# Second bucket pass: the first hop's pairs in runs of 3, 3, 3 instead of 2, 2, 2, 3

## The chip, the cores and the metric

One core of one Trainium2 chip. The metric is the device time of one execution in microseconds (us), lower is better. Engines are named as the profile names them: PE is TensorE (PEld its weight loads), DVE is VectorE, ACT is ScalarE, POOL is GpSimd, SP is SyncE, which here only issues DMAs.

## The reference, cut to what matters

```python
N, deg, D = 10000, 16, 128;  E = N * deg;  K = 7
h = x;  toks = [x]
for _ in range(K):
    msg = h[src] * deg_inv_sqrt[src, None] * deg_inv_sqrt[dst, None]
    h = _segment_sum(msg, dst, N)
    toks.append(h)
tok = jnp.stack(toks, axis=1)          # (N, K+1, D)
...                                    # one attention block over the 8 tokens of a node, then a weighted sum
```

Seven times, each of 10000 nodes sums the scaled rows of the nodes that point at it (160000 edges). The eight stages of a node then go through a small attention block. The change touches only the code that does the first of the seven sums.

## The kernel before, in words

**Stages.** A first bucket pass (`pass_a`) sorts the edges by the destination's tile of 128 nodes (79 tiles). A second bucket pass builds, for each destination tile, 0/1 matrices that gather source rows and scatter them, and stores them in DRAM. The first hop is done inside this second pass, tile by tile, with the matrices just built. Hops 2 to 7 read the matrices back (`run`, L738 on), and the attention block ends the kernel.

**The second pass in quads.** Tiles go in 20 groups of four (`quads`, L694; one has three). Three Python generators are advanced in turn in a loop of 16 steps per quad (L712 to 717):

- `place` (L418) for quad q+1. For each pair of tiles DVE makes a one-hot `oh` (L426), PE adds it up over 25 chunks into PSUM `ur` (L430), ACT casts to `H` (L431), PE multiplies by triangles (L436, "U"), ACT casts to `U2` (L438), DVE forms `ux` (L226), PE adds it up (L230, L231), DVE reduces to the ranks `rk` (L234), makes the one-hot `rob` (L441) and the two products `R` (L443, L444; L219), and PE multiplies `oh` by `R` into `tb` (50 matmuls, L449), which ACT casts to `tbs` (L450). `tbs` goes to DRAM as `srow` (L459). Then the overflow: `ct`, `cnt` matmul (L477), two one-hots `ohp` (L493) with 16 matmuls each (L496), `lo` (L499), `Sov` (L503).
- `matrices` (L506) for quad q, which is one quad ahead of hop 1. For each tile it reads a row of `srow`, broadcast, as `ra` and `rb` (L517); DVE compares `rb` (L524), ACT makes the next part from `ra` (L529), DVE the rest (L532); the tile `w` is written to DRAM (L534). `rb` has one buffer: the load for the next tile is issued by SP only when L524 of this tile is done.
- `hop1` (L697) for quad q-1: one `block` (L548) per tile.

**A block.** It has nine "pairs". `gather(jj)` (L602) is 8 matmuls with 32-column weights into a PSUM tile `p` (pool of three), L608, and one eviction to an SBUF tile `eb` by ACT (L613) or, in the last quad only, every second one by DVE (L615). `scat` (L575) is 4 matmuls with 128-column weights from `eb` into the accumulator (L558, L559). Gathers are issued in runs; after a run, pending scatters are issued until two are left (`lag`), so that a scatter follows its gather by a run. The generator yields after each run. When a block's last scatter is issued, `close` (L588) adds the rows that were fetched by indirect DMA and calls `fin1` (L676): DVE copies the in-degree (L677), ACT scales (L680, L651), and each second time the new table rows are made (L164, L165, L687).

**Buffers that matter here.** In `bw1` (one buffer each) the tags `ux` and `ohp` are shared: `ux` and `R` use one buffer, `ohp` and `rob` another. `oh` has three buffers.

**What sets the order.** The program order of the three generators gives priorities; a scheduler then decides the order of instructions on each engine when the program is built. Each engine runs its own list in order.

Of the kernel before, what the change touches and what calls it, by code (L numbers as in the profile page):

```python
# [47 lines left out]
class Hops:  # L48
# [608 lines left out]
    def run(self, ctx, att, nhop=K):  # L657
        tc, nc, V, A, T, G = self.tc, self.nc, self.nc.vector, self.nc.scalar, self.nc.tensor, self.nc.gpsimd
        with ExitStack() as c:
            self.bp = c.enter_context(tc.tile_pool(name="bp", bufs=1))  # L660
            self.TT = self.bp.tile([128, NCH, NTP], F32, name="TT")
            G.memset(self.TT[:, :, NK:], 0.0)
            self.pass_a()
            self.decode()
            self.gsp = c.enter_context(tc.tile_pool(name="gs1", bufs=6))
            self.pg = c.enter_context(tc.tile_pool(name="pg1", bufs=3, space=PSUM))
            self.pacc = c.enter_context(tc.tile_pool(name="pc1", bufs=2, space=PSUM))
            self.ogp = c.enter_context(tc.tile_pool(name="og1", bufs=2))
            self.fp = c.enter_context(tc.tile_pool(name="fp1", bufs=1))
            self.pb_open(c)  # L670
            pend = []

            done, stored = [], []


            def fin1(t, s, acc):  # L676
                V.tensor_copy(self.indeg[:, t:t + 1], acc[:, 128:129])  # L677
                if not done:
                    fin1.y = self.fp.tile([128, 2, 128], F32, name="y2")
                A.activation(fin1.y[:, len(done), :], s, AF.Copy, scale=self.dis2[:, t:t + 1])  # L680
                done.append(t)
                self.token_out(1, t, s, self.ctok[0])
                n, b = len(done), t + 1
                if n == 2 or b in (NT, 4 * NG):
                    a, new = b - n, self.tab[1]
                    self.to_table(fin1.y[:, :n, :], new, self.q2, a, b)
                    V.tensor_reduce(self.mx[1][:, a:b], new[:, a:b, 0:128], axis=X, op=ALU.max, apply_absolute_value=True)  # L687
                    stored.append((a, b))
                    done.clear()
                    while len(stored) > (t != last1):  # L690
                        self.rows(1, new, *stored.pop(0), nc.sync)


            quads = [list(range(a, min(NT, a + 4))) for a in (*range(4 * NG, NT, 4), *range(0, 4 * NG, 4))]  # L694
            dsl, W = [[] for _ in quads], [[] for _ in quads]

            def hop1(q):  # L697
                for t, w in zip(quads[q], W[q]):
                    og = [self.fetch(t, j, (self.tabd[0], self.tabh[0])) for j in range(NI + 1)]
                    yield from self.block(t, w, self.tab[0], og, pend, 2, (2, 2, 2, 3), True,  # L700
                                          lambda jj: q < nq - 1 or jj % 2 == 0, fin1, t == quads[0][0])

            nq, last1 = len(quads), quads[-1][-1]
            for _ in self.place(quads[0], dsl[0]):
                pass
            for q in range(nq + 1):
                pl = self.place(quads[q + 1], dsl[q + 1]) if q + 1 < nq else iter(())
                if q == 0:
                    mt = self.matrices(quads[0], dsl[0][0], W[0])
                    next(mt)  # L710
                hp = hop1(q - 1) if q else iter(())
                for i in range(16):  # L712
                    if i % 3 != 1:
                        next(pl, None)
                    if i % 4:
                        next(mt, None)
                    next(hp, None)
                for g in (pl, mt, hp):
                    for _ in g:
                        pass  # L720
                if q + 1 < nq:
                    mt = self.matrices(quads[q + 1], dsl[q + 1][0], W[q + 1])
                    next(mt)
            while pend:
                pend.pop(0)()
        with ExitStack() as c:
# [10 lines left out]
            pend = []  # L737
            for k in range(2, nhop + 1):  # L738
                i = 1 - k % 2
# [29 lines left out]
                og = [[None] * (NI + 1) for _ in order]  # L769
# [11 lines left out]
                for n, t in enumerate(order):  # L781
                    w = self.gsp.tile([128, (NJ + NG) * 128], F8, name="w")
# [591 lines left out]
```

## Time and profile before

| | |
|---|---|
| time, median of 3 | 3912.85 us (3900.72 to 3913.69) |
| the profiled execution | 3935.55 us, of which the span from first to last instruction is 3933.8 us |
| granted TensorE clock, mean | 0.977 |
| second bucket pass with hop 1 | about 410 to 1157 us of the span |
| hops 2 to 7 | from there to about 3290 us |
| busy share of the span | PE 94%, DVE 81%, ACT 72%, POOL 43% |

The profiled execution lies 0.6% above the median. In the rows of a timeline the columns are: start in us from the span's start, duration, engine, line, operation, output and input tiles, and in brackets how long the engine sat idle before it and what released it. In the table by windows each engine has its busy time and the number of its instructions, followed by the granted clock, the DMA share and GB/s.

### The profile page before, as it was taken

The page shows a single profiled execution, that of the slowest core. Times are in us where ns is not written, and L with a number is a line of the kernel's source. Part 1 is how long each engine was busy: PE and PEld are TensorE (multiplying, and loading weights), DVE is VectorE, ACT ScalarE, POOL GpSimd, SP SyncE. Part 2 cuts the span into 40 slices and gives each one's busy share as a digit, 9 for nine tenths or more (in the row PEclk, how much of TensorE's full clock was granted, in tenths as well). Part 3 has the DMA queues.
Part 4 walks back from the last instruction along what each step waited for, and adds up shares of the span by engine and source line. Part 5 has one row for each costly group of instructions (what it writes and reads, how often), then busy time and mean ns, then how long its engine had stood idle before and what let it go on. Part 6 is the DMA issues. An engine that isn't in the chain of part 4 may idle for free.

```text
span 3933.8 us, 174231 instructions
## 1 busy us (share of the span) xinstructions
PE 3693.9 (94%) x74141; PEld 2983.6 (76%) x74141; DVE 3172.3 (81%) x6888; ACT 2812.9 (72%) x6950; POOL 1678.8 (43%) x2221
## 2 busy tenths in 40 slices
PE   6786899999989999999999999999999998999997
PEld 4665677777768888888788788888878886777775
DVE  8998999999967777777777777777776664888888
ACT  6885577777766666766666667666765667888885
POOL 0000233323236665666666566656656662121111
PEclk8898899999999999999999999999999999999998
DMA  3100454544546666666666666666666552222220
GB/s 101 38 2 1 140 168 154 163 152 161 161 150 202 202 199 194 204 199 204 188 201 201 192 201 203 198 192 199 204 192 201 187 187 92 82 77 85 77 83 19
DMA packets 332729, 595.58 MB, mean 151 GB/s; under 512 B 57447, under 2 KB 215493, under 8 KB 326693
## 3 DMA queue, kind: packets, MB, share of 16 engines
q1 hardware_dynamic: 293989, 506.70, 40.0%
q0 software_dynamic: 35392, 72.55, 6.5%
q8 instruction: 580, 9.50, 1.0%
q10 hardware_dynamic: 2560, 5.12, 0.5%
q14 instruction: 208, 1.70, 0.1%
HBM read 455.49 MB, written 128.67 MB: 148 GB/s over the span
## 4 chain that ended last, share of the span: by engine, by line
PE 75%; DVE 14%; ACT 4%; DMA 4%; issue 2%; SPq 0%; another core or an unknown queue 0%; ACTq 0%; DVEq 0%; POOLq 0%
PE p L608 27%; PE acc L583 23%; PE acc L568 4%; PE pv L1018 4%; PE pu L1002 3%; DVE ux L226 2%; DVE o L219 2%; PE po L1037 2%; PE pt L992 2%; DVE oh L213 2%; PE tb L449 2%; DVE w L532 2%; PE ps L1067 1%; DVE R L219 1%; PE acc L558 1%
## 5 line engine op out<-in xcount | busy, mean ns | idle before, releaser
L613 ACT ACTIVATE eb<-p 128x512 f16<-128x512 f32 x3065 | 1638.7, 603 | 571.0 <-PE p L608 339.1
L615 DVE TENSOR_TENSOR eb<-p,four 128x512 f16<-128x512 f32 x1912 | 1230.9, 685 | 327.5 <-PE acc L583 189.7
L608 PE MATMUL p<-tab,w 128*32 128x256 f16 x39816 | 1291.8, 274 | 39.4 <-ACT eb L613 17.4
L608 PEld LDWEIGHTS <-w 128*32 128x32 fp8e4 x39816 | 997.5, 96 | 223.8 <-issue 169.2
L583 PE MATMUL acc<-eb,w 128*128 128x256 f16 x8532 | 1014.2, 273 | 0.5 <-issue 0.3
L583 PEld LDWEIGHTS <-w 128*128 128x128 fp8e4 x8532 | 836.9, 98 | 99.8 <-issue 1.0
L544 POOL DMA_INDIRECT og<-tabh,oidx x553 | 616.9, 1115 | 655.2 <-DVE oidx L468 394.5
L544 POOL DMA_INDIRECT og<-tabd,oidx x541 | 551.8, 1020 | 739.1 <-PE acc L566 359.6
L653 POOL TENSOR_SCALAR r<-s,ctok 128x128 f32<-128x128 f32 x474 | 294.8, 622 | 44.8 <-DVE s L599 27.8
L644 ACT ACTIVATE tab<-s,c 128x128 f16<-128x128 f32 x395 | 158.5, 401 | 198.0 <-DVE eb L615 171.4
L645 DVE SCALAR_TENSOR_TENSOR tab<-s,c,tab 128x128 f16<-128x128 f32 x395 | 138.9, 352 | 180.9 <-issue 168.3
L1107 POOL TENSOR_TENSOR p<-e,in 128x1024 f32<-128x1024 f32 (+1 forms) x40 | 76.5, 1914 | 446.6 <-DVE e L1106 446.6
L1059 ACT ACTIVATE junk<-tab 128x128 f32<-128x128 f32 x626 | 248.4, 401 | 8.2 <-SPq L1343 6.8
L347 ACT ACTIVATE rs<-iof,rb 128x128 fp8e4<-128x128 f32 x784 | 231.8, 391 | 0.3
L558 PE MATMUL acc<-eb,w 128*128 128x129 f16 x1422 | 214.2, 223 | 1.0 <-ACT w L529 0.9
L532 DVE TENSOR_TENSOR w<-dsl,iof 128x2432 fp8e4<-128x2432 f16 x79 | 211.9, 2682 | 2.7 <-PE acc L559 2.7
L599 DVE TENSOR_REDUCE s<-acc 128x128 f32<-128x256 f32 x474 | 196.3, 414 | 19.9 <-issue 8.9
L559 PE MATMUL acc<-eb,w 128*128 128x128 f16 x1422 | 210.1, 220 | 0.0
L543 POOL COPY og<-eb 128x1 f16<-128x1 f16 x452 | 84.0, 186 | 254.3 <-ACT eb L613 254.3
L558 PEld LDWEIGHTS <-w 128*128 128x128 fp8e4 x1501 | 139.2, 98 | 68.0 <-issue 64.3
L1018 PEld LDWEIGHTS pv<-Wv,xT 128*64 128x64 f32 x2504 | 138.8, 137 | 44.4 <-ACT uT L1003 29.7
L1018 PE MATMUL pv<-Wv,xT 128*64 128x131 f32 x2504 | 163.1, 280 | 8.6 <-issue 3.9
(299 smaller groups left out, 5033.1 us busy)
## 6 DMA issues: line engine op xcount, KB each, us to landing
w<-gsd SPq DMA_DIRECT2D x474, 592.0 KB
gsd<-w SPq DMA_DIRECT2D x79, 592.0 KB
tok<-r SPq DMA_DIRECT2D x546, 64.0 KB
tab<-tok SPq DMA_DIRECT2D x273, 128.0 KB
tabd<-tab SPq DMA_DIRECT2D x396, 64.0 KB
ra<-srow SPq DMA_DIRECT2D x79, 320.0 KB
rb<-srow SPq DMA_DIRECT2D x79, 256.0 KB
og<-tabh,oidx POOLq DMA_INDIRECT x553
```

What stands on the lines that cost most here:

```text
L347: A.activation(ro[:, j - a, i, :], self.iof, AF.Abs_reciprocal_sqrt, scale=2.0 ** 21, bias=rb[:, j - VP, i:i + 1], saturate=False)
L532: V.tensor_tensor(w[:, :NJ * 128].rearrange("p (j d) -> p j d", d=128), dsl[:, g, :, None].to_broadcast([128, NJ, 128]), self.iof1[:, None ...
L544: self.nc.gpsimd.indirect_dma_start(out=o, out_offset=None, in_=src[0] if i == NI else src[1], in_offset=bass.IndirectOffsetOnAxis(ap=self ...
L558: T.matmul(acc[0][:, :128 + ones], W, rows[:, 128:256 + ones], start=start, stop=False, skip_group_check=True)
L559: T.matmul(acc[0][:, :128], W, rows[:, :128], start=False, stop=False, skip_group_check=True)
L583: T.matmul(acc[0][:, :256], w[:, J * 128:(J + 1) * 128], e[:, j, :256], start=False, stop=J == NG - 1 and not late)
L608: T.matmul(p[32 * q:32 * q + 32, j], w[:, NJ * 128 + s * CAP:NJ * 128 + (s + 1) * CAP], tab[:, s, :], start=True, stop=True)
L613: A.activation(e[:, :n, 0:256], pv, AF.Copy, scale=4.0)
L615: V.tensor_tensor(e[:, :n, 0:256], pv, self.four[:, :, None].to_broadcast([128, n, 256]), op=ALU.mult)
L653: self.nc.gpsimd.tensor_scalar(r, s, ct[:, t:t + 1], None, op0=ALU.mult)
L1018: T.matmul(p[64 * h:64 * h + 64, u - us[0], :], S[i]["xT"][:, h * m + q, 64 * c:64 * c + 64], Wv, start=True, stop=True, tile_position=(0, ...
L1059: A.activation(j, S[i]["x"][:, g, :], AF.Square, bias=S[i]["x"][:, g, 0:1], scale=-1.0, accum_out=R[i % 6][:, 0, g:g + 1])
```

## The change

In the first hop, the nine gathers of a block are issued in runs of 3, 3, 3 instead of 2, 2, 2, 3. A block then yields three times instead of four, and `hop1` is advanced in 12 of the 16 steps of a quad instead of in all of them. Nothing is computed differently.

```diff
             def hop1(q):
                 for t, w in zip(quads[q], W[q]):
                     og = [self.fetch(t, j, (self.tabd[0], self.tabh[0])) for j in range(NI + 1)]
-                    yield from self.block(t, w, self.tab[0], og, pend, 2, (2, 2, 2, 3), True,
+                    yield from self.block(t, w, self.tab[0], og, pend, 2, (3, 3, 3), True,
                                           lambda jj: q < nq - 1 or jj % 2 == 0, fin1, t == quads[0][0])
...
                     if i % 4:
                         next(mt, None)
-                    next(hp, None)
+                    if i % 4 != 3:
+                        next(hp, None)
                 for g in (pl, mt, hp):
                     for _ in g:
                         pass
```

Since a scheduler sets the order on each engine, the change moves more than the gathers. After some irregular first quads, the order before repeats itself quad by quad; the order of the change repeats itself every two quads, six times (quads 6 to 17). Call these two quads A and B. The three places below are all in that steady part.

DVE around the first `tb` of a quad: `R` is the last input of the `tb` matmuls, L524 is the compare of `rb`, and the 128x3800 rows are `oh` and `ux`. Before:

```order
L219 TENSOR_TENSOR R<-rob,dl 128x25x64
L454 MAX ov<-vo 128x8 x2
L524 TENSOR_SCALAR w<-rb,pid_232 128x1024
L213 TENSOR_TENSOR oh<-kB,io_230 128x3800
L226 TENSOR_TENSOR ux<-oh,U_14861 128x3800
L677 COPY indeg<-acc 128x1
L524 TENSOR_SCALAR w<-rb,pid_232 128x1024
```

The same place in the change, quad A:

```order
L219 TENSOR_TENSOR R<-rob,dl 128x25x64
L454 MAX ov<-vo 128x8 x2
L524 TENSOR_SCALAR w<-rb,pid_232 128x1024
L226 TENSOR_TENSOR ux<-oh,U_14861 128x3800
L677 COPY indeg<-acc 128x1
L524 TENSOR_SCALAR w<-rb,pid_232 128x1024
```

and quad B:

```order
L219 TENSOR_TENSOR R<-rob,dl 128x25x64
L454 MAX ov<-vo 128x8 x2
L226 TENSOR_TENSOR ux<-oh,U_15812 128x3800
L677 COPY indeg<-acc 128x1
L524 TENSOR_SCALAR w<-rb,pid_232 128x1024
```

`oh` has left this place (it now stands between `rk` and `rob` further on); `ux` follows instead, in A with one L524 ahead of it and in B with none. In A only `ux` and a copy are left between two L524.

DVE behind the second `tb`, where the matrices of the next quad begin (L532 is the long compare of `matrices`, `po` and `ph` belong to the overflow). Before:

```order
L468 TENSOR_SCALAR oidx<-msc 128x4
L532 TENSOR_TENSOR w<-dsl,iof_228 128x2432
L480 TENSOR_TENSOR po<-msc,iof_228 128x32
L524 TENSOR_SCALAR w<-rb,pid_232 128x1024
L481 TENSOR_TENSOR po<-po,fl 128x32
L483 TENSOR_SCALAR ph<-po 128x4x8
L213 TENSOR_TENSOR ohp<-ph,io_230 128x2048
L677 COPY indeg<-acc 128x1
L532 TENSOR_TENSOR w<-dsl,iof_228 128x2432
L213 TENSOR_TENSOR ohp<-ph,io_230 128x2048
```

In the change, end of quad A:

```order
L468 TENSOR_SCALAR oidx<-msc 128x4
L532 TENSOR_TENSOR w<-dsl,iof_228 128x2432
L480 TENSOR_TENSOR po<-msc,iof_228 128x32
L524 TENSOR_SCALAR w<-rb,pid_232 128x1024
L481 TENSOR_TENSOR po<-po,fl 128x32
L532 TENSOR_TENSOR w<-dsl,iof_228 128x2432
L483 TENSOR_SCALAR ph<-po 128x4x8
L677 COPY indeg<-acc 128x1
L524 TENSOR_SCALAR w<-rb,pid_232 128x1024
L213 TENSOR_TENSOR ohp<-ph,io_230 128x2048
```

The second L524 of the quad stands one L532 and three small rows behind the first; before, it came a dozen rows further on, behind `Sov`. In B the second L524 stands far behind, as it did before.

ACT around the first `tb` (`tbs` is cast when the `tb` matmuls are done, `U` when the triangle matmuls of L436 are done, `H` when those of L430 are). Before:

```order
L431 CAST H<-ur 128x152
L613 ACTIVATE eb_256<-p 128x2x256
L613 ACTIVATE eb_258<-p 128x2x256
L613 ACTIVATE eb_260<-p 128x2x256
L450 CAST tbs<-tb 76x128
L438 CAST U_14861<-ur 128x152
```

In the change, quad B:

```order
L431 CAST H<-ur 128x152
L613 ACTIVATE eb_264<-p 128x2x256
L438 CAST U_15812<-ur 128x152
L613 ACTIVATE eb_256<-p 128x2x256
L450 CAST tbs<-tb 76x128
```

PE's order is the same in this: before, L430, gathers, `tb`, scatters, triangles; now L430, triangles, gathers, `tb`. The triangles, which need `H`, have moved ahead of `tb`, in A as in B.

## The prediction

> **What bounds the kernel now.** I read the busy table first, then the windows, then the waits of the engine that looks full, then its timeline. The change can act only in the second bucket pass, so the averages of the span are not what counts.
>
> ```profile
> PE 3693.9 (94%) x74141; PEld 2983.6 (76%) x74141; DVE 3172.3 (81%) x6888; ACT 2812.9 (72%) x6950; POOL 1678.8 (43%) x2221
> ```
>
> By this PE is the fullest engine. In a window of one steady quad of the second pass (37.3 us) and one near its end, it is otherwise:
>
> ```profile
> 600.00:640.00 40.00, 37.04 (x756) 29.26 (x749) 39.66 (x55) 31.01 (x66) 17.29 (x9) 0.96 0.49 164
> 832.00:869.30 37.30, 34.97 (x718) 27.54 (x715) 34.89 (x52) 29.12 (x62) 11.45 (x8) 1.00 0.50 160
> 1125.00:1140.00 15.00, 13.55 (x283) 9.38 (x279) 5.00 (x14) 11.94 (x26) 4.03 (x6) 1.00 0.34 102
> ```
>
> DVE (third column) works 34.89 of 37.30 us with 52 instructions. PE shows as much, but the ends of its overlapping matmuls are modelled, so a full column is not a full engine; what decides is who waits. In the earlier, irregular quads (first row) DVE has only 0.34 us free in 40. At the end (third row) DVE is a third busy and PE and ACT carry the work. The steady stretch of ten quads, 740 to 1110 us, has these waits, of DVE and then of PE (total, times, longest):
>
> ```profile
> DVE oh L213 <- PE tb L449: 18.6, 17, 1.7
> DVE w L524 <- DMA rb<-srow: 5.2, 8, 1.6
> DVE oidx L468 <- ACT dsl L467: 4.1, 2, 2.1
> DVE ux L226 <- ACT U L438: 3.3, 1, 3.3
> ...
> PE tb L449 <- DVE R L219: 8.8, 11, 1.0
> PE p L608 <- ACT eb L613: 5.0, 10, 0.7
> ```
>
> DVE waits 31.2 us of 370, most of it for PE to finish the 50 `tb` matmuls, and PE in turn stands at `tb` until DVE has written `R`. One quad of DVE's timeline shows it:
>
> ```profile
> 890.15 0.68 DVE L503 TENSOR_TENSOR Sov<-lo,iof 128x512 fp8e4<-128x512 f32 x1
> 894.08 0.41 DVE L234 TENSOR_REDUCE rk<-ur 128x50 f16<-128x250 f32 x1
> 896.46 0.98 DVE L219 TENSOR_TENSOR R<-rob,dl 128x1600 f16<-128x1600 f16 x1
> 897.54 0.73 DVE L524 TENSOR_SCALAR w<-rb,pid 128x1024 fp8e4<-128x1024 f16 x1
> 899.53 2.14 DVE L213 TENSOR_TENSOR oh<-kB,io 128x3800 f16<-128x3800 f16 x1 [1.25 <-PE tb L449]
> 901.58 2.17 DVE L226 TENSOR_TENSOR ux<-oh,U 128x3800 f16<-128x3800 f16 x1
> 903.74 0.74 DVE L524 TENSOR_SCALAR w<-rb,pid 128x1024 fp8e4<-128x1024 f16 x1
> ...
> 913.21 2.14 DVE L213 TENSOR_TENSOR oh<-kB,io 128x3800 f16<-128x3800 f16 x1 [0.88 <-PE tb L449]
> 915.34 2.68 DVE L532 TENSOR_TENSOR w<-dsl,iof 128x2432 fp8e4<-128x2432 f16 x1
> 918.26 0.75 DVE L524 TENSOR_SCALAR w<-rb,pid 128x1024 fp8e4<-128x1024 f16 x1
> ...
> 927.42 0.68 DVE L503 TENSOR_TENSOR Sov<-lo,iof 128x512 fp8e4<-128x512 f32 x1
> ```
>
> From `Sov` to `Sov` a quad takes 37.27 us, of which DVE waits 1.25 + 0.88 = 2.13 us. So **DVE's own list sets the pace** of the steady quads: a quad is its work (35.1 us) plus what it waits. PE's side of the first wait:
>
> ```profile
> 894.79 1.82 PE L430 MATMUL ur<-oh,id 128*128 128x152 f16 x25
> 897.50 1.99 PE L449 MATMUL tb<-R,oh 128*76 128x64 f16 x50
> ```
>
> `R` ends at 897.44, `tb` starts at 897.50 and ends at 899.49, `oh` starts at 899.53. The L524 between (0.66 us from start to next start) only fills part of those 2 us.
>
> **The change part by part.** No engine gets an instruction more or less; DVE's 35.1 us per quad stay. What changes is how often PE turns from 32-column to 128-column weights, and the order.
>
> *Turns on PE: four per block become three.*
>
> ```profile
> 825.24 0.62 PE L608 MATMUL p<-tab,w 128*32 128x256 f16 x16
> 825.79 0.23 PE L558 MATMUL acc<-eb,w 128*128 128x129 f16 x1
> ...
> 827.50 0.22 PE L558 MATMUL acc<-eb,w 128*128 128x129 f16 x1
> 827.56 0.22 PE L559 MATMUL acc<-eb,w 128*128 128x128 f16 x1
> 827.71 0.40 PE L608 MATMUL p<-tab,w 128*32 128x256 f16 x8
> ...
> 831.21 0.84 PE L608 MATMUL p<-tab,w 128*32 128x256 f16 x24
> 831.98 0.23 PE L558 MATMUL acc<-eb,w 128*128 128x129 f16 x1
> ```
>
> From the start of 16 gather matmuls to the next scatter it is 0.55 us, of 24 it is 0.77: 0.22 us for each eight and 0.11 once. From the last scatter back to a gather it is 0.15 us, where two scatters are 0.06 apart: 0.09. A turn there and back costs 0.20 us; 79 blocks save 79 x 0.20 = 16 us of PE. **DVE's list hides it**: PE already stands waiting for `R`. Only where DVE is not the bound does it show: in about the last 45 us, of which the third window is a part, some six blocks of 7 us: 6 x 0.20 = **1.2 us gained**. The Trainium skill, "TensorEngine Tiling (Array Packing)", section "Key Properties", says that changing the tiling mode drains TensorE; the 0.20 us a turn agree with that, and by that rule alone the sum would be the 16 us of the rival below, by the waits it is 1.2.
>
> *The wait for the first `tb`.* `oh` leaves this place, but `ux` takes it, and `ux` is written into the buffer that holds `R` until `tb` has read it: the same wait, under another name. In A the L524 still stands between, so it stays about 1.25 us. In B it does not: the wait grows by its 0.66 us. **0.66 us lost per two quads.** The second wait (0.88 us) keeps the same rows ahead of it.
>
> *The distance between two L524.* `rb` has one buffer, so L524 of the next tile waits for a load that SP can issue only after this L524. What that load takes, the trace shows where L524 waited:
>
> ```profile
> 854.79 0.38 SPq L517 DMA_DIRECT2D rb<-srow  x1
> 860.58 0.75 DVE L524 TENSOR_SCALAR w<-rb,pid 128x1024 fp8e4<-128x1024 f16 x1 [0.45 <-DMA rb<-srow]
> 877.62 0.32 SPq L517 DMA_DIRECT2D rb<-srow  x1
> 881.14 0.75 DVE L524 TENSOR_SCALAR w<-rb,pid 128x1024 fp8e4<-128x1024 f16 x1 [0.47 <-DMA rb<-srow]
> ```
>
> 3.5 us on a quiet queue, 5.8 us behind other loads. Between the two L524 at the end of A stand one L532 (2.6 us) and three small rows (0.5 us): 3.1 us. Before, the next one stood behind `Sov`, more than 9 us on (918.26 to 927.42). DVE will wait 0.4 to 2.7 us; I take 1.0, nearer the short load, since the `ra` loads ahead of it are 3 us old by then. At the head of A the gap is the `tb` wait (1.25), `ux` (2.05) and a copy: 3.4 us, where it was 5.5 (897.54 to 903.74, less its own 0.66). DVE will wait 0.1 to 2.4 us; here I take 0.8. **Together 1.8 us lost per two quads.** Queued behind a waiting L524 is all of DVE's list: `ohp` and with it PE's 16 matmuls, or the table rows.
>
> Against this, some of the old 5.2 us of such waits fall in places that now have more room; I count 2 us gained once.
>
> *The order on PE and ACT.* The triangles now stand ahead of `tb`, and need `H`. From the end of `rk` (894.49), which frees `ur`, to the end of `R` is 2.95 us. In that time PE must do L430 (1.75), get `H` from ACT (about 0.45 with the latency), do the triangles (0.2) and part of a run of gathers (0.4): 2.8 us. It just fits, as it just fitted before (`tb` started 0.06 us behind `R`). I take 0, with the bounds 0 and three evictions of 0.54 us queued ahead of `H`, 1.6 us per quad.
>
> *The irregular quads before the steady part* are reordered as well. DVE is free 0.34 us in 40 there, so over some eight quads 3 us can be gained at most; lost would be 10 us, if each of them lost what a steady one does (2.46 / 2). The row with next to no free time is the nearer one, and I take 0.
>
> **The sum.** Six pairs of quads: 6 x (0.66 + 1.8) = 14.8 us lost; 1.2 and 2 gained; 11.6, say **+11 us**. The profiled execution has 3935.55 us (span 3933.8 and 1.75 around it), so 3946.6 there. It lies 0.6% above the median of the runs shown, 3912.85; since the sum is a difference, I put it on the median: **3924 us**.
>
> **The rivals.**
>
> *PE sets the pace.* For it speaks PE's 94%. Then the turns count in full: 16 us less, 3897 us. Against it: PE waits for `R`, not DVE for anything but the chain that begins with `R`. If the first `oh` wait went as well (ten quads, half of 18.6 us), 3912.85 - 16 - 12 = 3885; but `ux` shares its buffer with `R`, which forbids it.
>
> *Nothing moves.* The scheduler puts different rows at the same waits and `rb` always lands in time: 6 x 0.66 - 3.2 = +1, 3914 us.
>
> *`rb` comes late* (slower). Place: the second L524 at both spots of A. At the 5.8 us load DVE waits 2.7 and 2.4 us: 6 x (0.66 + 5.1) - 3.2 = +31, 3944 us. It decides from the point where the loads take more than about 4.9 us: then the two waits add up to 3.2 us and the loss passes 0.5%. For it: gathers by POOL and stores of 592 KB share the engines, and SP issues in order. Against it: at 903.74 a load with 5.5 us of room caused no wait.
>
> *`tb` comes late* (slower). Place: the triangles ahead of `tb`. If ACT has evictions queued ahead of `H`, DVE waits for each tenth. At the full 1.6 us in twelve quads it is 19 us more, with 0.66 kept and 1.8 halved: +25, 3938 us.
>
> **How the numbers follow.** Chances: forecast 0.45, nothing moves 0.12, PE sets the pace 0.06 and with the `oh` wait gone too 0.06, `rb` late 0.18, `tb` late 0.13. 0.5% (20 us) is about what a measurement of this kernel can tell from no change: faster than 3893, or slower than 3932. Faster: 0.06. Slower: the two slow rivals and 0.05 of the forecast's upper end, 0.36. Same: 0.58. The range leaves out the fastest case and a little beyond the slow ones: 3895 to 3952.
>
> **What would show it.** In the changed profile: `ux` (L226) instead of `oh` waits for `tb`, about 1.25 and 1.9 us in alternate quads; L524 waits for `rb` about twice per two quads with a sum near 14 us in the steady part, where it was 5.2; PE's `tb` still waits for `R`; two quads take about 77 us from `Sov` to `Sov` instead of 74.5; DVE's busy time unchanged. The prediction is wrong if PE has no wait left at `tb` (then PE leads and the turns count), if a quad is shorter than 37.27 us, or if L524's waits stay at 5 us.

## The result, and the profile after

The change takes 3919.45 us (median of 20 runs, 3908.87 to 3928.08) against 3911.36 us of the kernel before (20 runs, 3900.72 to 3913.87): a ratio of **1.0024 [1.0017, 1.0031]**, which is 6.6 to 12.1 us more. The prediction was 3924 us, 11 more than before. The profiled execution of the change took 3922.04 us (span 3920.0, clock 0.973). That of before was a long one, so the two spans can't be compared; the second pass can. The rows of the tile `Sov` give each instruction's first and last start, here of the last matmul of a block and of `Sov` itself. Before, then the change:

```profile
L566 PE MATMUL acc<-ones,Sov x79: 164/167/211, 426.0 to 1155.3; 128*128 128x1 f16 x79
L503 DVE TENSOR_TENSOR Sov<-lo,iof x20: 547/684/689, 421.0 to 1111.6; 128x512 fp8e4<-128x512 f32 x19, 128x384 fp8e4<-128x384 f32 x1
```

```profile
L566 PE MATMUL acc<-ones,Sov x79: 165/167/211, 425.3 to 1168.0; 128*128 128x1 f16 x79
L503 DVE TENSOR_TENSOR Sov<-lo,iof x20: 559/684/689, 419.1 to 1126.5; 128x512 fp8e4<-128x512 f32 x19, 128x384 fp8e4<-128x384 f32 x1
```

From the first `Sov` to the end of hop 1, which I call the **stretch** below, it was 734.3 us and is 748.9: 14.6 us more. From the last `Sov` to the end it was 43.7 and is 41.5: the tail gained 2.2. So the quads lost 16.8 us. The stretch is of one execution of each kernel: over the kernels of the table below, what it lies above that of before differs from what the ratio gives by -3 to 14 us (here 14.6 against 9.4), so smaller differences of single stretches carry little.

The waits of DVE and then of PE, 740 to 1110 us of the change (us in total, times, longest):

```profile
DVE ux L226 <- PE tb L449: 12.1, 5, 3.0
DVE w L524 <- DMA rb<-srow: 11.2, 17, 2.1
DVE oh L213 <- PE tb L449: 8.9, 8, 1.9
DVE ux L226 <- issue: 6.7, 5, 1.4
DVE lo L499 <- PE msc L496: 2.6, 4, 0.7
...
PE acc L558 <- ACT eb L613: 13.4, 10, 3.6
PE tb L449 <- DVE R L219: 12.4, 9, 1.9
PE msc L496 <- DVE ohp L213: 6.3, 5, 2.1
```

As forecast, `ux` stands where `oh` stood at the first `tb` (five times with the releaser `tb`, five times in quads A under "issue"), and the waits for `rb` have doubled. DVE waits 43.8 us in all, where it was 31.2. A row that the prediction did not have leads PE's list: scatters (`acc`, L558) that wait for an eviction, 13.4 us; before, the view had no such row. PE waits 34.3 us in all, where it was 25.3.

The timeline shows the two kinds of wait of `ux`, first in a B, then in an A:

```profile
749.20 0.98 DVE L219 TENSOR_TENSOR R<-rob,dl 128x1600 f16<-128x1600 f16 x1
753.36 2.14 DVE L226 TENSOR_TENSOR ux<-oh,U 128x3800 f16<-128x3800 f16 x1 [2.99 <-PE tb L449]
...
791.64 2.14 DVE L226 TENSOR_TENSOR ux<-oh,U 128x3800 f16<-128x3800 f16 x1 [1.33 <-issue]
```

```profile
751.21 2.05 PE L449 MATMUL tb<-R,oh 128*76 128x64 f16 x50
```

In this B, `R` ended at 750.18 and `tb` began only at 751.21, after the triangles and gathers: it is 1.03 us late on top of the forecast's 1.9. Over the five quads B the wait is 12.1 / 5 = 2.4 us; the last two of them wait 1.98 and 1.99, with `tb` 0.05 us behind `R`.

A late `rb` costs more than DVE's own wait. Of DVE, ACT and PE about 852 us:

```profile
848.81 0.32 SPq L517 DMA_DIRECT2D rb<-srow  x1
...
852.32 0.85 DVE L524 TENSOR_SCALAR w<-rb,pid 128x1024 fp8e4<-128x1024 f16 x1 [2.09 <-DMA rb<-srow]
853.19 0.14 DVE L677 COPY indeg<-acc 128x1 f32<-128x1 f32 x1
853.37 0.37 ACT L680 ACTIVATE y<-acc,dis 128x128 f32<-128x128 f32 x1 [2.60 <-DVE indeg L677]
855.00 1.57 ACT L613 ACTIVATE eb<-p 128x512 f16<-128x512 f32 x3
855.64 0.22 PE L558 MATMUL acc<-eb,w 128*128 128x129 f16 x1 [3.65 <-ACT eb L613]
856.06 1.47 PE L608 MATMUL p<-tab,w 128*32 128x256 f16 x24
```

Read it downward: L524 waits 2.09 us for `rb`; the copy of the in-degree stands behind it; ACT's L680 waits 2.60 us for that copy; the evictions stand behind L680; and PE's scatter waits 3.65 us for the first of them. With runs of three and two scatters left pending, the third scatter issued after a run belongs to that run's own first pair, so PE needs an eviction that has only just become possible. With runs of two that happens only in the run of three that ends a block.

The last row has a second surprise: 24 gather matmuls in 1.47 us, where they took 0.84. The granted clock is the number in the third column from the right. After an idle of 1.97 us that ends at 738.94:

```profile
739.00:741.00 2.00, 2.00 (x44) 1.37 (x44) 2.00 (x4) 0.92 (x3) 0.00 (x0) 0.68 0.48 161
741.00:743.00 2.00, 2.00 (x36) 1.95 (x33) 2.00 (x4) 2.00 (x4) 0.00 (x0) 0.50 0.68 238
743.00:745.00 2.00, 2.00 (x38) 1.54 (x37) 2.00 (x4) 1.51 (x5) 1.69 (x2) 0.96 0.44 178
```

```profile
738.94 0.56 PE L496 MATMUL msc<-dg,ohp 128*128 128x3 f16 x16 [1.97 <-DVE ohp L213]
739.67 1.45 PE L608 MATMUL p<-tab,w 128*32 128x256 f16 x24
```

The clock is at half for some 3 us. I summed (1 - clock) over windows of 2 us from 440 to 1156: the change loses 25.6 us of clock, before lost 8.5.

### The profile page after: what moved, and what is told of

Its sections match the earlier page's. It is cut to its first block, busy times and chain, and to the rows that moved or that the text cites. A ratio compares the mean times of both kernels' runs of the same rounds, so it can differ in the third digit from the quotient of the medians.

```text
span 3920.0 us, 174223 instructions
## 1 busy us (share of the span) xinstructions
PE 3681.7 (94%) x74141; PEld 3000.7 (77%) x74141; DVE 3163.4 (81%) x6888; ACT 2763.6 (71%) x6950; POOL 1724.6 (44%) x2221
## 4 chain that ended last, share of the span: by engine, by line
PE 66%; DMA 2%; DVE 1%; ACT 1%; issue 0%; POOL 0%; SPq 0%; POOLq 0%; ACTq 0%; DVEq 0%
PE p L608 24%; PE acc L583 23%; PE acc L568 4%; PE pv L1019 4%; PE pu L1003 4%; PE po L1038 2%; PE pt L993 2%; PE ps L1068 1%; DMA og<-tabd,oidx 1%; PE pf L1227 1%; PE sm L1074 1%; PE pf L1053 0%; DMA tabd<-tab 0%; ACT junk L1060 0%; DVE eb L615 0%
## 5 line engine op out<-in xcount | busy, mean ns | idle before, releaser
L613 ACT ACTIVATE eb<-p 128x512 f16<-128x512 f32 x3065 | 1586.7, 607 | 581.7 <-PE p L608 563.2
L615 DVE TENSOR_TENSOR eb<-p,four 128x512 f16<-128x512 f32 x1912 | 1190.5, 683 | 306.0 <-PE p L608 303.1
L608 PE MATMUL p<-tab,w 128*32 128x256 f16 x39816 | 1264.6, 275 | 8.4 <-DMA tabd<-tab 4.4
L544 POOL DMA_INDIRECT og<-tabh,oidx x553 | 641.5, 1160 | 626.5 <-DVE oidx L468 393.9
L583 PEld LDWEIGHTS <-w 128*128 128x128 fp8e4 x8532 | 835.8, 98 | 102.5 <-issue 4.7
L544 POOL DMA_INDIRECT og<-tabd,oidx x541 | 573.5, 1060 | 546.5 <-PE acc L559 311.8
L645 DVE SCALAR_TENSOR_TENSOR tab<-s,c,tab 128x128 f16<-128x128 f32 x395 | 169.1, 428 | 180.5 <-ACT tab L644 180.5
L558 PE MATMUL acc<-eb,w 128*128 128x129 f16 x1422 | 218.7, 225 | 27.8 <-ACT eb L613 27.6
L532 DVE TENSOR_TENSOR w<-dsl,iof 128x2432 fp8e4<-128x2432 f16 x79 | 211.9, 2683 | 2.5 <-PE acc L559 2.5
L599 DVE TENSOR_REDUCE s<-acc 128x128 f32<-128x256 f32 x474 | 196.5, 415 | 17.3 <-PE acc L597 13.5
L558 PEld LDWEIGHTS <-w 128*128 128x128 fp8e4 x1501 | 143.0, 99 | 49.6 <-issue 46.9
L559 PEld LDWEIGHTS <-w 128*128 128x128 fp8e4 x1501 | 149.0, 99 | 32.0 <-issue 31.5
```

The source lines that it names most:

```text
L532: V.tensor_tensor(w[:, :NJ * 128].rearrange("p (j d) -> p j d", d=128), dsl[:, g, :, None].to_broadcast([128, NJ, 128]), self.iof1[:, None ...
L544: self.nc.gpsimd.indirect_dma_start(out=o, out_offset=None, in_=src[0] if i == NI else src[1], in_offset=bass.IndirectOffsetOnAxis(ap=self ...
L558: T.matmul(acc[0][:, :128 + ones], W, rows[:, 128:256 + ones], start=start, stop=False, skip_group_check=True)
L559: T.matmul(acc[0][:, :128], W, rows[:, :128], start=False, stop=False, skip_group_check=True)
L583: T.matmul(acc[0][:, :256], w[:, J * 128:(J + 1) * 128], e[:, j, :256], start=False, stop=J == NG - 1 and not late)
L608: T.matmul(p[32 * q:32 * q + 32, j], w[:, NJ * 128 + s * CAP:NJ * 128 + (s + 1) * CAP], tab[:, s, :], start=True, stop=True)
```

## The experiments

**Theory 1**, the prediction's: DVE's list sets the pace, and its new order (`ux` at `tb`, close L524 with a late `rb`, and what stands behind them) makes the loss. **Theory 2**: the runs of three make it, because scatters wait for evictions of their own run. **Theory A**: the falls of the clock make it. **The rival to theory 1**: PE sets the pace. Every edit moves the order on all engines, so a ratio alone is not the price of the edit, and each kernel is read by its own trace. The ratios are to the kernel before on the same chip; stretch and sums of waits (740 to 1110 us) are of one profiled execution.

| kernel | ratio, 95% interval | stretch, us | DVE waits | PE waits | clock lost, us |
|---|---|---|---|---|---|
| before | 1 | 734.3 | 31.2 | 25.3 | 8.5 |
| the change | 1.0024 [1.0017, 1.0031] | 748.9 | 43.8 | 34.3 | 25.6 |
| e1_rb2_after | 1.0018 [1.0008, 1.0028] | 752.3 | 40.5 | 43.2 | 17.1 |
| e2_rb2_before | 1.0006 [0.9996, 1.0016] | 745.0 | 36.4 | 26.4 | 18.8 |
| e3_loop_only | 1.0016 [1.0008, 1.0025] | 746.3 | 40.2 | 20.6 | 11.9 |
| e4_runs_only | 1.0066 [1.0051, 1.008] | 774.3 | 53.2 | 43.4 | 25.6 |
| e5_L524_twice | 1.009 [1.0075, 1.0104] | 770.9 | 22.8 | 38.9 | 25.6 |
| e6_gathers_again | 1.0152 [1.0137, 1.0166] | 790.5 | 54.3 | 35.1 | 3.4 |
| e7_keep_clock | 1.0035 [1.0023, 1.0046] | 752.4 | 45.5 | 34.4 | 25.6 |
| e8_lag_three | 1.0026 [1.0016, 1.0036] | 743.7 | 35.8 | 34.1 | 20.5 |
| e9_before_gathers | 1.0163 [1.0147, 1.0178] | 806.8 | 56.4 | 25.1 | 10.2 |
| e10_other_skip | 1.0011 [1.0002, 1.002] | 744.5 | 36.8 | 36.4 | 23.9 |
| e11_skip_and_lag | 0.9994 [0.9985, 1.0004] | 734.7 | 29.5 | 32.2 | 10.3 |
| e12_before_L524 | 1.0083 [1.0066, 1.0101] | 780.5 | 24.5 | 31.4 | 25.7 |

### The halves of the change, and a second `rb`

**e1 and e2**, the change and before with two buffers for `rb`:

```diff
-        es = cp.tile([NS, 4, NJ], I32, name="es")
+        es = self.bw1.tile([NS, 4, NJ], I32, name="es", tag="ux")
...
-            rb = self.bw1.tile([128, 4 * NG * CAP - m], F16, name="rb")
+            rb = self.bwp.tile([128, 4 * NG * CAP - m], F16, name="rb")
```

> The change, with two buffers for rb instead of one (the setup tile es shares another buffer to make room). The scheduler now gives every quad the order of quad B. Theory 1 (the loss is the chain that begins where L524 waits for rb: DVE waits, the in-degree copy behind it, ACT's y behind that, the evictions behind y, PE's scatter behind those, and then the TensorE clock drops): L524's waits for rb, 11.2 us in 740 to 1110 us in the change, go below 2 us; PE's waits of its scatters for evictions over 1.5 us go; time 3905 to 3913 us. Theory 2 (the runs of three themselves cost, since a run's last scatter needs an eviction of the same run): the waits of scatters for evictions stay, 3917 to 3925 us. Theory 3 (PE waits 2 us for the first ohp in each B quad, and its clock drops behind that): the drops now come in every quad, 3917 to 3930 us.

> The kernel before, with two buffers for rb. Theory 1: its waits of L524 for rb (5.2 us in ten quads) go, with few other things to gain: 3903 to 3911 us. Theories 2 and 3 say nothing of it but what a new order does, 3908 to 3920 us.

**e3 and e4**, each half of the change alone: the skipped step with runs of 2, 2, 2, 3, and runs of 3, 3, 3 with all 16 steps.

> One half of the change alone: hop 1 is advanced in 12 of 16 steps, with runs of 2, 2, 2, 3; the last four runs of a quad are issued behind the loop. Theory 2: no run of the same length waits for its own evictions, so as before, 3907 to 3915 us. Theory 1: what counts is how far apart two L524 come to stand, which in this order is again 3 to 5 us at some places: rb waits of 5 to 12 us in the steady part, 3912 to 3928 us.

> The other half alone: runs of 3, 3, 3, advanced in all 16 steps (so hop 1 of a quad is issued in the first twelve). Theory 2: as the change, 3916 to 3923 us. Theory 1: in this order a quad has three pairs of L524 that stand close together (in front of rob and behind R; at the quad's end), so rb waits grow beyond the change's 11.2 us: 3920 to 3940 us.

The waits of e1:

```profile
DVE w L524 <- DMA rb<-srow: 5.3, 6, 1.9
...
PE acc L558 <- ACT eb L613: 23.0, 11, 3.4
```

The second buffer halves the waits for `rb` (11.2 to 5.3), not to nothing. The scatters' waits do not go with them; they grow to 23.0 us. So the late `rb` of the chain above is one way to such a wait, not its cause, and nothing certain is gained (1.0018 against 1.0024). Before gains nothing either.

Both halves alone are slower than before. In e3, with runs of two, PE's wait of scatters is nearly absent while `ux` waits for `tb`; in e4 it is the other way round. e3, then e4:

```profile
DVE ux L226 <- PE tb L449: 21.8, 10, 2.5
...
PE acc L558 <- ACT eb L613: 1.2, 1, 1.2
```

```profile
DVE rk L234 <- PE ur L231: 17.3, 9, 1.9
...
PE acc L558 <- ACT eb L613: 25.1, 28, 3.0
```

That ties the first mechanism to the skipped step's order and the waits of scatters to the runs of three. The 1.0066 of e4 is not the price of its scatters' waits alone: its order also makes DVE wait 15.9 us for `rb` and 17.3 us for `ur`. The second of these comes from DVE's order, as the next section shows.

### Which engine sets the pace

**e5** (on the change) and **e12** (on before) issue every L524 twice:

```diff
             V.tensor_scalar(w[:, cut:], rb, self.pid1, 0.25, op0=ALU.is_equal, op1=ALU.mult, saturate=False)
+            V.tensor_scalar(w[:, cut:], rb, self.pid1, 0.25, op0=ALU.is_equal, op1=ALU.mult, saturate=False)
```

> The change, with every L524 of the second pass issued twice (79 more DVE rows of 0.66 us from start to next start, 52 us of DVE work in all). Theory 1, DVE's list sets the pace of the second pass: the span grows by 40 to 60 us against the change (ratio to before 1.012 to 1.018), and the quads grow from 39.0 to about 41.6 us. Rival, PE sets the pace: DVE has 4 to 5 us of waits per quad into which 2.6 us fit, the span grows by 0 to 15 us (ratio 1.002 to 1.006), and the DVE waits of the steady stretch fall by about 25 us.

> The kernel before, with every L524 of the second pass issued twice as in e5_L524_twice (52 us more of DVE work in all, 2.64 us per quad). Theory 1, DVE's list sets the pace before and a row added to it can at most fill its waits of 3.2 us per quad: if the added rows stand where DVE does not wait, 40 to 55 us more (ratio 1.010 to 1.014); if they fill the waits for tb, 15 to 30 us more, as in e5 (26 us more than the change), and DVE's waits in the steady stretch fall from 31 us to 15 or less. Rival, PE sets the pace before: 0 to 10 us more (ratio 1.000 to 1.003), and DVE's waits fall by about 25 us.

**e6** (on the change) and **e9** (on before) issue the first pair's gathers of each block four times:

```diff
-                    T.matmul(p[32 * q:32 * q + 32, j], w[:, NJ * 128 + s * CAP:NJ * 128 + (s + 1) * CAP], tab[:, s, :], start=True, stop=True)
+                    for _ in range(4 if first and jj == 0 else 1):
+                        T.matmul(p[32 * q:32 * q + 32, j], w[:, NJ * 128 + s * CAP:NJ * 128 + (s + 1) * CAP], tab[:, s, :], start=True, stop=True)
```

> The change, with the eight gather matmuls of the first pair of each block issued four times (24 more rows of 0.0275 us each per block, 0.66 us, 52 us of PE work in all; the result is written again, nothing else changes). Theory 1, DVE's list sets the pace: PE has 4 to 6 us of waits per quad, so most of it is hidden: 5 to 25 us more than the change (ratio to before 1.004 to 1.009), through a longer wait for tb where the added rows stand ahead of it. Rival, PE sets the pace: 40 to 55 us more (ratio 1.012 to 1.017).

> The kernel before, with the same added gather matmuls as in e6_gathers_again (52 us of PE work). DVE's order in the steady quads is that of e6_gathers_again row for row, so the two differ in the runs alone. Theory 1, DVE's list sets the pace before: 5 to 25 us more than before (ratio 1.001 to 1.006). Rival, PE paces the quads as much as DVE: 40 to 65 us more (ratio 1.010 to 1.017). Against e6_gathers_again (ratio 1.0152): if the saved turns count, this one is 8 to 16 us longer than e6 (ratio 1.017 to 1.019); if the waits of scatters for the evictions of their own run eat them up, it is the same or shorter (ratio 1.013 to 1.016).

52 us of added DVE work cost 26 us on the change ((1.009 - 1.0024) x 3911) and 32 on before. The kernels with 52 us of added PE work are 50 and 64 us longer. By the ratios alone theory 1 would fall here: PE would not be hidden. But all four edits also gave DVE a new order, and e9 loses more than the work that was added, so the traces have to say what was paid for. e6, waits of DVE and PE, then e5, waits of DVE:

```profile
DVE rk L234 <- PE ur L231: 18.0, 9, 2.0
DVE oh L213 <- PE tb L449: 7.5, 8, 1.0
DVE w L524 <- PE acc L559: 6.7, 9, 1.9
DVE lo L499 <- PE msc L496: 5.9, 9, 0.7
DVE ohp L213 <- PE msc L496: 5.9, 9, 0.7
...
PE tb L449 <- DVE R L219: 10.0, 9, 1.1
PE ur L230 <- DVE ux L226: 2.9, 10, 0.5
```

```profile
DVE w L524 <- DMA rb<-srow: 14.2, 16, 2.1
DVE lo L499 <- PE msc L496: 7.9, 7, 2.1
DVE ohp L213 <- PE msc L496: 0.7, 2, 0.6
```

In e6 `rk` waits 2.0 us for `ur` in each of nine quads. In the steady quads of before and of the change, five to seven rows stand between `ux` and `rk` in DVE's list; in e6 and e9 there is none once per quad (in e4 there is one). One such place in e6, DVE and then PE:

```profile
876.21 2.13 DVE L226 TENSOR_TENSOR ux<-oh,U 128x3800 f16<-128x3800 f16 x1
880.34 0.42 DVE L234 TENSOR_REDUCE rk<-ur 128x50 f16<-128x250 f32 x1 [2.00 <-PE ur L231]
```

```profile
878.39 1.81 PE L230 MATMUL ur<-ux,id 128*128 128x250 f16 x15
```

`ux` ended at 878.34 and PE began at 878.39: the added gathers were not in the way, and PE itself waits for `ux` here (2.9 us in ten times). The waits of `oh`, `ohp` and `lo` in e6 are of the same kind. By the timelines PE began 0.05 or 0.06 us behind the row that it needed, at every one of them. Together these are 37.3 of DVE's 54.3 us. In e9 they are 38.6 of 56.4, and PE began within 0.09 us. PE comes late at two other places: where L524 waits for a `w` that the scatters have not yet freed (6.7 us in e6, 7.3 in e9), and where `ux` waits for `U`, which follows PE's triangles (3.0 and 6.3). That is at most 9.7 and 13.6 us, where 9 x 2.64 = 24 us of PE work were added. Nor did that work fill PE's own waits: 35.1 us in e6 and 34.3 in the change, 25.1 in e9 and 25.3 before.

So e6 and e9 show above all a price of DVE's order. **Theory 1's bound, DVE's list, stands, and the rival, that PE sets the pace, is not borne out**; what added PE work would cost in an unchanged order stays open. In e5 the added L524 stand partly where DVE waited for `tb` anyway: those waits are gone from its list, as are the 18.6 us of before in e12, where more waits for `rb` (16.7 us) take a part of them back.

From the seventh `Sov` on, e6 and e9 have the same DVE order row for row, so there they differ in the runs. From the eighth to the eighteenth `Sov` a quad takes 41.11 us in e6 and 41.77 in e9. Of the 0.66 us between them, 0.36 is the wait of `ux` for `U`; four turns at 0.20 us are 0.80. So in this order a part of PE's saved turns does reach DVE. The Trainium skill, "TensorEngine Tiling (Array Packing)", "Key Properties", has a change of tiling mode drain TensorE; that the kernel with fewer turns has the shorter quads agrees, but does not show the drain by itself. By the ratios the difference is smaller (1.0163 against 1.0152) and the intervals overlap, so in the whole time it is not resolved.

### The clock, the pending scatters and the order

**e7**, 16 small matmuls to keep PE busy ahead of `ohp`:

```diff
+        for _ in range(16):
+            T.matmul(msc[:, 108:128], self.id16, ph.rearrange("p k g -> p (k g)")[:, :20], start=True, stop=True)
```

> The change, with 16 small matmuls of 20 columns (into columns of msc that nothing reads, inputs id16 and ph) ahead of the first 16 matmuls that take ohp, so that PE is not idle while it waits for ohp. Theory A, the clock that falls to half behind an idle of over 1.6 us costs time in the change: the falls behind the waits for ohp are gone, the lost clock (25 us in the change between 440 and 1156 us) is 15 or less, and the time is 3 to 8 us less than that of the change (ratio to before 0.9995 to 1.001). Rival B, the slow matmuls behind a fall lie beside DVE's list: the falls are gone and the time stays within 3 us of the change (ratio 1.0017 to 1.003).

PE's longest waits in e7, the lines being two further down in this kernel:

```profile
PE acc L560 <- ACT eb L615: 18.4, 11, 2.4
```

The waits for `ohp` are gone, but those for evictions have grown and the clock falls behind them: 25.6 us lost, as in the change. It did not make the state that it was to test, so it **decides nothing about theory A**. Against a large price speaks e2: it loses 10.3 us more of clock than before, and its ratio of 1.0006 has an interval that spans 1.

**e8**, three pending scatters instead of two, so that no scatter needs its own run's eviction:

```diff
-        self.more_ebufs(cp, 5)
+        self.more_ebufs(cp, 6)
...
-                    yield from self.block(t, w, self.tab[0], og, pend, 2, (3, 3, 3), True,
+                    yield from self.block(t, w, self.tab[0], og, pend, 3, (3, 3, 3), True,
...
-            self.more_ebufs(c.enter_context(tc.tile_pool(name="eb2", bufs=1)), 9, False)
+            self.more_ebufs(c.enter_context(tc.tile_pool(name="eb2", bufs=1)), 8, False)
```

> The change, with three pending scatters left after each run of three instead of two (and six eb buffers in the second pass instead of five), so that no scatter needs an eviction of its own run. Theory 2, the scatter of the run's own first pair is what the runs of three cost: the waits of scatters for eb (13.4 us in the steady stretch of the change) fall below 3, the falls of the clock behind them are gone, and the time is 3 to 9 us less than that of the change (ratio to before 0.9995 to 1.0015). Rival, PE's waits are hidden by DVE's list: the waits for eb are gone as well, but DVE's waits of the stretch stay above 40 us and the time is within 3 us of the change (ratio 1.0017 to 1.003).

**e10**, another step skipped:

```diff
-                    if i % 4 != 3:
+                    if i % 4 != 0:
```

> The change, with hop1 left out in the first of every four steps instead of the last (i % 4 != 0). The runs are 3, 3, 3 and the turns as few as in the change, while DVE's order in the steady quads is nearly that of before (oh at the first tb, L524 between R and oh). Theory 1 as predicted (DVE's order makes the loss): the waits of ux for tb and the close L524 are gone, the steady quad is 37.3 to 37.8 us as before, the ratio is 0.9985 to 1.0005. Theory 2 (the runs of three make the loss): PE's waits for eb stay at 10 us or more in the steady stretch, the clock falls behind them, and the ratio is 1.002 to 1.004. A third, PE's saved turns count once DVE's order is that of before: 8 to 16 us less than before, ratio 0.996 to 0.998.

**e11**, both together.

> e10_other_skip together with the three pending scatters and six eb buffers of e8_lag_three. DVE's order is nearly that of before, the turns are those of the change, and no scatter needs an eviction of its own run. Theory 1 (DVE's order alone makes the loss): as e10, ratio 0.9985 to 1.0005. Theory 2 (the evictions of the own run make it): shorter than e10 by 5 to 12 us and shorter than before, ratio 0.996 to 0.999. If neither counts and PE's waits only move to another place (gathers for a free p): ratio 1.001 to 1.004.

The waits of DVE and PE, of e8, e10 and e11:

```profile
DVE ux L226 <- PE tb L449: 5.9, 3, 2.0
...
PE tb L449 <- DVE R L219: 15.2, 14, 1.9
PE p L608 <- ACT eb L613: 9.0, 11, 1.5
```

```profile
DVE oh L213 <- PE tb L449: 16.6, 17, 2.1
DVE w L524 <- DMA rb<-srow: 6.3, 10, 1.2
...
PE tb L449 <- DVE R L219: 12.6, 15, 1.1
PE acc L558 <- ACT eb L613: 9.0, 13, 1.3
```

```profile
DVE oh L213 <- PE tb L449: 15.9, 17, 2.0
...
PE tb L449 <- DVE R L219: 9.7, 11, 0.9
...
PE p L608 <- ACT eb L613: 5.9, 11, 1.0
```

In e8 the scatters' waits for `eb` are gone; 9.0 us of gathers that wait for a free `p` take their place, `ux` still waits for `tb`, and the time is that of the change (1.0026). That is the rival's case, though DVE's waits are 35.8 us and not above 40. In e10 DVE's first wait is `oh` again and `rb` waits 6.3 us, nearly as before, while the scatters' waits stay at 9.0; the ratio, 1.0011, lies between the two theories' numbers. In e11 both are gone: a stretch of 734.7 us against 734.3 of before, and 5.4 us less than e10 on the same chip (3908.12 against 3913.52 us).

So **both theories seem to carry a part**: of the change's 9 us (0.0024 x 3911), about 5 go when DVE has nearly its old order (1.0024 to 1.0011), and the rest, with 2 more, when the scatters no longer need their own run (1.0011 to 0.9994). The intervals of neighbours touch, so these shares are rough; only those of the change and of e11 lie well apart. The second part seems to be had only after the first: e8, which does it alone, gains nothing. How scatters on PE reach DVE can be read from the timelines. Where DVE waits for `tb`, `ur` or `msc`, the time by which PE began behind the row that it needed (at most the wait) is 1.7 us in all before, 5.8 in the change, 8.9 in e10 and 5.0 in e11. From e10 to e11 the clock lost falls as well, from 23.9 to 10.3 us, so theories 2 and A are not separated by this step. e11 ties with the kernel before, its interval spanning 1; none of these kernels beats both.

## Why the prediction was right, and where its steps were not

**The time** was right: 8 us more by the medians where 11 were forecast. The terms:

- **The wait for the first `tb`**: `ux` took the place of `oh`. In A 6.7 / 5 = 1.3 us (forecast 1.25), in B 2.4 (forecast 1.9). "I take 0" for the triangles ahead of `tb` was too little: `tb` started up to 1.03 us after `R`. The size lies inside the bounds of that term.
- **The distance between two L524**: the waits for `rb` rose by 11.2 - 5.2 = 6.0 us in the steady stretch, where 14 - 5.2 = 8.8 were forecast.
- **The tail**: 2.2 us gained, forecast 1.2.
- **The irregular quads**, "I take 0": from the first to the eighth `Sov` it was 243.3 us before and is 250.4, 7.1 us more. DVE's waits for `rb` from 420 to 740 us went from 1.1 to 9.2. The row with next to no free time was no reason to take 0; it had room for new waits.
- **The pace**: ten quads (from the eighth `Sov`) took 37.6 us each before and take 39.0. Two quads take 78.0 us where 77 were forecast; they took 75.2, so they lost 2.8 where 2.46 were forecast. DVE's own work per quad stayed: 37.6 less 31.2/370 of it, and 39.0 less 43.8/370, are both 34.4 us. The last two intervals between `Sov` took 71.1 us and take 67.1: 4.0 us gained that the forecast did not have.

The bound, "**DVE's own list sets the pace**" with "**DVE's list hides it**", held for the change. Of its 18 waits of `ux` and `oh` for `tb`, 14 had PE begin 0.05 us behind `R`. In e11, with fewer turns than before and nearly the same DVE order, the stretch stays the same and PE's waits rise from 25.3 to 32.2 us, 6.9 us, where the saved turns of ten quads are 10 x 4 x 0.20 = 8. It need not hold in every order, as e6 against e9 shows.

The step that failed is what the new order costs on PE: "It just fits [...] I take 0". The prediction looked for losses on DVE alone. It missed that PE's lateness reaches DVE (5.8 us of DVE's waits, 1.7 before), in part at `lo`, which waits 2.6 us for `msc` and had no such row before. And it did not have the scatters that wait for the evictions of their own run (13.4 us on PE) or the falls of the clock. That its sum came out is partly luck: the loss of the irregular quads, taken at 0, was made up by the gain in the last quads and by `rb` waits that it had set too high. One of its rivals has a slip: half of 18.6 us is 9.3, or 11 for twelve quads, not 12; 3885 would be 3888 or 3886, which changes no chance.

Still open: what the falls of the clock cost by themselves, since e7 did not remove them, and what PE work costs when DVE's order stays. Which part of the irregular quads' loss belongs to which cause was not tried.

## What to carry to other kernels

When two engines wait for each other, a wait does not yet say which of them is late. Look whether the releaser began as soon as its input was there: if it did, the order of the waiting engine is the cause, and rows put between its two ends would fill the wait. An edit that adds work can change that order too, so read the trace of the edited kernel before taking its ratio for the price of the work. When runs of work are lengthened, lengthen the number of pending items with them; otherwise the consumer asks for an item of the run that has just been issued (here the time seemed to follow only once DVE's order was mended too). Where a cheap instruction of one engine's list stands behind a wait, follow who needs it: here a late load reached PE through a copy on DVE and a scaling on ACT.

## What the runs showed of the hardware

An idle of 1.97 us on PE was followed by a fall of the granted clock to 0.50, for 3.41 us by the trace's clock record. In the change, thirteen idles of 1.6 to 3.65 us lie in the second pass from 640 us on. Twelve were followed by such a fall; one of 1.87 us, ending at 1050.84, was not. Idles of 1.50 us or less were followed by none there, but in e10 one of 1.33 us, ending at 659.67, was. Before, the longest idle from 640 to 1110 us was 1.88 us, and no fall followed it. So length alone does not decide.

Where an idle lies counts too. The falls of the change all start on one grid of 3.41 us. I summed PE's idle from 640 to 1110 us in each cell of that grid: the twelve cells ahead of a fall hold 1.62 us or more, all others at full clock 1.50 or less, and before none holds over 1.51. The idle of 1.87 us without a fall is split over two cells, 1.38 and 0.49. In other kernels the two groups overlap (in e1 a cell of 0.83 us stands ahead of a fall, one of 1.72 does not), so these runs give no threshold.

The Trainium skill, "TensorE: Matmul & The Clock Gate", Part 1, gives half rate after at least one idle window of about 3.4 us; here less than 2 us of idle sufficed, and the measurement decides. Its release after about 3.4 us of sustained activity agrees with the 3.41 us seen here.
